# Six head blocks' memory V turned by a transposing DMA instead of TensorE, in a long one-core kernel

## The chip, the cores and the metric

The kernel runs on one core of a Trainium2 chip. The metric is the device time of one execution in microseconds (us). Each kernel is run several times, in rounds beside the kernel before on the same chip. Single runs of one kernel agree within about 0.1%.

In the profiles PE is TensorE (matmuls), PEld its weight loads, DVE VectorE, ACT ScalarE, POOL GpSimd, and SP the engine (SyncE) whose queue issues most DMAs. A q after an engine's name, as in SPq, means its sequencer, which waits, branches and issues DMAs. PSUM is the memory that the matmuls here write to (tiles psP, psO, psS, psU, psR), SBUF the one that holds the other on-chip tiles.

## The reference, cut to what matters

The program computes two independent things and joins them: a state-space layer (A) and a recurrent attention with memory (B). Only B matters here.

```python
for s in range(n_seg):                       # 64 segments of 32 rows
    h = jnp.concatenate([mem, xs], axis=1)   # 8 memory rows and 32 rows of x
    q, k, v = h @ Wq, h @ Wk, h @ Wv         # 32 heads of 128
    p = softmax(mask(q @ k.T * scale))
    o = (p @ v) @ Wo
    mem = o[:, :M, :]                        # memory of the next segment
    outs.append(o[:, M:, :])
```

The kernel doesn't walk through the 64 segments. It guesses all memory rows first (73 distinct ones in all), computes all segments at once, and checks the guess at the end. If the check failed, a slow general loop would run; it is in the program as a branch that is skipped in these runs.

## The kernel before

The 32 heads are worked in 16 pairs (`hp`), and V in 8 blocks of four heads (`hb`). V of the x rows is computed in the first phase and kept in DRAM (`vx`). V of the 73 memory rows is computed by `v_mem`: for blocks 0 and 1 at the end of the second phase, for blocks 2 to 7 inside the attention phase.

```python
def v_mem(self, hb, w=None):
    k = self.k
    w = w or self.load_wv(hb)
    p = k.ps("P")
    for h in range(4):
        for c in range(KC):
            k.PE.matmul(p[:, h * NM:(h + 1) * NM], w[:, c, h * 128:(h + 1) * 128], self.memT[:, c, :], start=(c == 0), stop=(c == KC - 1))
    vm = self.vmp.tile([128, 4, NM], BF16, name="b_vm", bufs=1)
    k.copy("v", vm[:], p[:, 0:4 * NM].rearrange("p (h n) -> p h n", h=4))
    yield
    pt = k.ps("P", (128, 1024), BF16)
    for h in range(4):
        k.PE.transpose(pt[0:NM, h * 128:(h + 1) * 128], vm[:, h, :], k.ident[:])
    st = self.next_st()
    k.copy("v", st[0:NM, 0, :, 0:E], pt[0:NM, 0:512].rearrange("p (h e) -> p h e", h=4))
    sv = st[:, 0, :, :].rearrange("p h e -> p (h e)")
    k.SP.dma_start(self.vx[hb][64:64 + NMX, :], sv[0:NMX, :])
    k.SP.dma_start(self.vt[hb][:], sv[NMX:NM, :])
    yield
```

The result lies with the head's 128 elements on the partitions and must be turned, so that the rows can be stored. TensorE does it, four transposes a block. In the attention phase the steps of this generator are interleaved with the rest, and the V tile of the next head pair is loaded from DRAM some way behind:

```python
for n, (hp, u) in enumerate(at):                 # at: attention, 11 steps u for each head pair
    ...
    if hp % 2 == 0 and 2 < hp + 2 < HP:
        if u == 4:
            vm = b.v_mem(hp // 2 + 1)
        if u in (4, 6):
            next(vm)
    ...                                          # projections of the next pair are mixed in here
```

## Time and profile before

| | before |
|---|---|
| time, median of 3 runs (lowest to highest) | 1247.11 us (1246.69 to 1247.39) |
| span of the profiled execution | 1245.3 us |
| TensorE (PE) busy | 1234.2 us, 99% |
| VectorE (DVE) busy | 667.7 us, 54% |

These are lines of the page of the kernel before: busy time of each engine, then the chain of waits that ended last, by engine and by line.

```profile
span 1245.3 us, 20124 instructions
PE 1234.2 (99%) x8270; PEld 662.5 (53%) x8342; DVE 667.7 (54%) x1250; ACT 263.4 (21%) x631; POOL 275.8 (22%) x407
...
PE 99%; issue 0%; DVE 0%
```

TensorE is the limit nearly everywhere. In the ten windows of 50 us from 550 to 1050 us it is busy 499.74 of 500 us.

What does one group of transposes cost? The timeline of PE around the first of the six groups says it (start in us, length in us, engine, line, operation, tiles, shape, count):

```profile
570.71 0.33 PE L64 MATMUL psO<-b_v,b_m 128*128 128x129 bf16 x3
570.88 0.39 PE L64 MATMUL psP<-ident,b_vm 128*73 128x128 bf16 x4
571.10 1.55 PE L64 MATMUL psP<-b_xe,b_wk 128*128 128x201 bf16 x16
```

The lengths overlap: four transposes of 219 ns each take 0.39 us together. The starts don't overlap: from 570.88 to 571.10 is 0.22 us for four transposes.

The queue of SP in the same stretch, kernel before (one row is one DMA's issue, waits included):

```profile
566.98 0.54 SPq L64 DMA_DIRECT2D b_wq<-in_B_Wq_dram  x1
568.82 0.39 SPq L64 DMA_DIRECT2D b_wk<-in_B_Wk_dram  x1
571.92 0.30 SPq L64 DMA_DIRECT2D b_vx<-b_vst  x1
572.27 0.32 SPq L64 DMA_DIRECT2D b_vt<-b_vst  x1
572.64 0.30 SPq L64 DMA_DIRECT2D b_tn<-b_ob  x1
572.98 0.40 SPq L64 DMA_DIRECT2D b_wv<-in_B_Wv_dram  x1
589.03 2.01 SPq L64 DMA_DIRECT2D b_on<-b_ob  x2
```

After 573.4 us the queue does nothing until 589.0 us: there is room.

### The profile page before, as it was taken

What the parts mean: (1) busy time and instruction counts of PE and PEld (TensorE: products, weight loads), DVE (VectorE), ACT (ScalarE), POOL (GpSimd) and SP (SyncE); (2) the same over time, 40 slices, a digit from 0 to 9 for tenths busy, and PEclk for the clock granted to TensorE, in tenths of its full rate; (3) what the DMA queues carried; (4) which work ended last, traced back from release to release, by engine and by line L of the source; (5) the groups of instructions that cost most, each with busy time, mean ns of one, the idle gap of its engine ahead of it and who ended that gap; (6) DMA issues with size and microseconds to landing.
All of it is one profiled execution on the core that took longest, in us unless ns stands there. A gap on an engine that the chain in (4) does not pass through costs nothing.

```text
span 1245.3 us, 20124 instructions
## 1 busy us (share of the span) xinstructions
PE 1234.2 (99%) x8270; PEld 662.5 (53%) x8342; DVE 667.7 (54%) x1250; ACT 263.4 (21%) x631; POOL 275.8 (22%) x407
## 2 busy tenths in 40 slices
PE   9999999999999999999999999999999999999998
PEld 5444444444455555556666656555665554446444
DVE  4688899998711124666666666666666641001000
ACT  5344444443310000211112111111211110000000
POOL 4111331212332321322222222222222220000000
PEclk9999999999999999999999999999999999999999
DMA  9965444554898734664454545545553379407000
GB/s 248 272 191 147 131 135 127 144 155 107 242 322 248 249 116 95 196 170 124 96 145 108 144 108 120 132 92 121 120 142 92 65 211 230 107 18 153 17 26 19
DMA packets 316246, 176.83 MB, mean 142 GB/s; under 512 B 138874, under 2 KB 301550, under 8 KB 316150
## 3 DMA queue, kind: packets, MB, share of 16 engines
q1 hardware_dynamic: 294054, 147.95, 47.8%
q10 hardware_dynamic: 21072, 24.38, 5.9%
q0 software_dynamic: 1024, 3.17, 0.7%
q8 instruction: 66, 1.08, 0.4%
q14 instruction: 30, 0.25, 0.1%
HBM read 89.14 MB, written 53.17 MB: 114 GB/s over the span
## 4 chain that ended last, share of the span: by engine, by line
PE 99%; issue 0%; DVE 0%
PE psP L64 82%; PE psU L64 9%; PE psS L64 3%; PE psO L64 2%; PE psR L64 2%; DVE b_xe L91 0%; DVE b_ost L91 0%; DVE a_n L962 0%; DVE hpb L105 0%; DVE ones L102 0%
## 5 line engine op out<-in xcount | busy, mean ns | idle before, releaser
L64 PE MATMUL psP<-b_xe,b_wq 128*128 128x480 bf16 (+1 forms) x1280 | 247.7, 343 | 0.1
L64 PE MATMUL psP<-b_xe,b_wk 128*128 128x480 bf16 (+1 forms) x1280 | 247.7, 343 | 0.0
L64 PE MATMUL psP<-b_wv,b_xe 128*128 128x512 bf16 (+2 forms) x1033 | 223.4, 372 | 0.8
L644 POOL TENSOR_TENSOR b_m<-b_e,maskB 99x396 bf16<-99x396 bf16 x160 | 139.8, 874 | 338.5 <-ACT b_e L641 338.5
L641 ACT ACTIVATE b_e<-psS 99x396 bf16<-99x396 f32 x176 | 88.2, 501 | 536.7 <-PE psS L64 533.4
L64 PEld LDWEIGHTS <-b_wk 128*128 128x128 bf16 x1280 | 119.4, 98 | 94.2
L64 PEld LDWEIGHTS <-b_wq 128*128 128x128 bf16 x1280 | 118.7, 98 | 87.7
L64 PEld LDWEIGHTS <-b_xe 128*128 128x128 bf16 x1056 | 101.8, 98 | 119.1 <-DVE b_xe L91 0.2
L91 DVE CAST b_k<-psP 128x480 bf16<-128x480 f32 (+1 forms) x192 | 97.4, 528 | 100.9 <-PE psP L64 100.9
L91 DVE CAST b_q<-psP 128x480 bf16<-128x480 f32 (+1 forms) x192 | 97.4, 528 | 93.1 <-PE psP L64 91.5
L64 PEld LDWEIGHTS <-b_ol 128*128 128x128 bf16 x864 | 84.3, 98 | 94.4
L64 PE MATMUL psU<-a_xT,a_bt 128*128 128x512 bf16 x493 | 113.9, 379 | 1.1
L64 PE MATMUL psP<-t,a_hl 128*128 128x512 bf16 x496 | 112.1, 379 | 0.8
L91 DVE CAST b_ost<-psP 128x512 bf16<-128x512 f32 (+1 forms) x17 | 11.5, 676 | 177.4 <-PE psP L64 176.3
L64 PE MATMUL psP<-wo,b_ol 128*128 128x512 bf16 (+1 forms) x440 | 91.9, 364 | 0.4
L64 PE MATMUL psP<-t,b_ol 128*128 128x512 bf16 x408 | 91.7, 379 | 0.4
L280 POOL TENSOR_SCALAR a_tt<-a_pr,a_tabf 128x1 f32<-128x1 f32 x48 | 34.1, 710 | 243.2 <-DVE a_pr L275 243.2
L661 DVE TENSOR_TENSOR b_ob<-psO,b_accR 99x384 bf16<-99x384 f32 x160 | 85.9, 553 | 2.4 <-DVE b_accR L660 0.4
L89 ACT ACTIVATE b_vst<-psP 128x512 bf16<-128x512 f32 x126 | 71.9, 589 | 71.3 <-PE psP L64 59.9
L267 DVE TENSOR_TENSOR a_pr<-psU,a_tabf 128x2048 f32<-128x2048 f32 x32 | 73.0, 2282 | 15.7 <-PE psU L64 14.0
L64 PEld LDWEIGHTS <-a_bt 128*128 128x128 bf16 x512 | 49.2, 98 | 57.6
L64 PEld LDWEIGHTS <-a_hl 128*128 128x128 bf16 x512 | 49.0, 98 | 56.7
(200 smaller groups left out, 962.7 us busy)
## 6 DMA issues: line engine op xcount, KB each, us to landing
b_v<-b_vx SPq DMA_DIRECT2D x16, 1122.0 KB
b_wv<-in_B_Wv_dram SPq DMA_DIRECT2D x16, 1024.0 KB
b_vx<-b_vst ACTq DMA_DIRECT2D x24, 544.0 KB
b_on<-b_ob SPq DMA_DIRECT2D x15, 720.0 KB
a_hs<-a_h SPq DMA_DIRECT2D x32, 256.0 KB
b_wog<-in_B_Wo_dram SPq DMA_DIRECT2D x4, 2048.0 KB
b_wq<-in_B_Wq_dram SPq DMA_DIRECT2D x16, 512.0 KB
b_wk<-in_B_Wk_dram SPq DMA_DIRECT2D x16, 512.0 KB
```

The costliest lines, as they stand in the source:

```text
L64: r = f(*a, **kw)
L89: self.S.activation(out, in_, ACT.Copy)
L91: self.V.tensor_copy(out, in_)
L267: V.tensor_tensor(pr[:], u[:].unsqueeze(1).to_broadcast([128, 2, 2, TB]), view(t3, [[TB + 1, 2], [TB + 1, 2], [1, TB]]), ALU.mult)
L280: G.tensor_scalar(tt[:, j:j + 1], w[:, j, TB - 1:TB], t3[:, 1, TB:TB + 1], None, ALU.mult)
L641: k.S.activation(e[:], s[0:GW, :, :, 0:GW], ACT.Exp, scale=float(E) ** -0.5, accum_out=self.accE[0:GW, i:i + 1])
L644: k.G.tensor_tensor(m[0:GW, 0:4 * GP].rearrange("p (a b q) -> p a b q", a=2, b=2)[:, :, :, 0:GW], e[:], mask[0:GW, :, :].unsqueeze(2).to_b ...
L661: V.tensor_tensor(self.ob[:, b0:b0 + n, :], o[0:GW, 0:n, 0:E], r.unsqueeze(2).to_broadcast([GW, n, E]), ALU.mult)
```

## The change

The intent is to take the 24 transposes of blocks 2 to 7 off TensorE, which is the limit, and give them to the DMA engines, which are nearly half idle (on the page of the kernel before the packets take 54.9% of the time of 16 engines, the sum of its five queues). The transposing DMA of this program reads from DRAM, so the tile is stored there first.

```diff
+        self.vmt = [k.drp.tile([E, 512], BF16, name=f"b_vmt{i}") for i in range(HB)]
 ...
-        vm = self.vmp.tile([128, 4, NM], BF16, name="b_vm", bufs=1)
-        k.copy("v", vm[:], p[:, 0:4 * NM].rearrange("p (h n) -> p h n", h=4))
+        vm = self.vmp.tile([128, 4, 128], BF16, name="b_vm", bufs=1)
+        k.copy("v", vm[:, :, 0:NM], p[:, 0:4 * NM].rearrange("p (h n) -> p h n", h=4))
+        if hb > 1:
+            k.V.memset(vm[:, :, NM:128], 0.0)
+            k.SP.dma_start(self.vmt[hb][:], vm[:].rearrange("p h n -> p (h n)"))
+            yield
+            s = self.next_st()[:].rearrange("p i h e -> p (i h e)")[:, 0:576].rearrange("p (h e) -> p h e", h=4)
+            k.V.memset(s[:, :, E:EW], 1.0)
+            k.SP.dma_start_transpose(s[:, :, 0:E], self.vmt[hb][:])
+            yield
+            k.SP.dma_start(self.vx[hb][64:64 + NMX, :].rearrange("n (h e) -> n h e", h=4), s[0:NMX, :, 0:EW])
+            k.SP.dma_start(self.vt[hb].rearrange("n (h e) -> n h e", h=4), s[NMX:NM, :, 0:EW])
+            yield
 ... (the old way stays for blocks 0 and 1; for blocks 2 to 7 the generator is advanced three times and never gets there)
-                if u in (4, 6):
+                if u in (4, 6, 8):
                     next(vm)
```

Note two things that the intent doesn't mention. The SBUF tile `b_vm` grows from 584 to 1024 bytes in each partition. And SP gets 23 instructions more (583 to 606 in the built main block; twelve DMAs and their waits).

## The prediction

> **What bounds the kernel now.** TensorE. The page gives PE 1234.2 us busy of a 1245.3 us span (99%), granted clock 0.999; the chain of waits is 99% PE. In ten 50 us windows from 550 to 1050 us (most of the attention phase) PE is busy 499.74 of 500 us, DVE 60%, POOL 27%, ACT 18%, DMA about half. In the waits of 480 to 960 us no PE row appears: DVE, ACT and POOL wait for PE, never the reverse. So PE time removed there should come off the total one for one, and nothing else should.

> **What the change removes.** For head blocks 2 to 7: four TensorE transposes each (24 in all, with their weight loads) and one 391 ns DVE copy from PSUM. The trace gives 219 ns for one transpose, but that is a pipelined length. The PE timeline shows what the group occupies: transposes start at 570.88 us, the next projection matmul at 571.10 us; the other five blocks read the same (638.45 to 638.67, and so on). So 0.22 us per block, 1.3 us in all, 55 ns per transpose. [...] Multiplying 24 by 219 ns would give 5.3 us, which I take to be wrong.

> **What it adds.** Per block, on the SP queue: a 128 KB store to DRAM, one transposing DMA that waits for it, and the two V stores cut into 272-byte instead of 1088-byte runs, waiting for the transpose. On DVE: two small memsets. The built order of PE instructions differs only by the 24 transposes; ACT and POOL are identical.

> **Is the added latency on the path?** Before, the V stores issue at 571.9 and 572.3 us, and the next V load that can read them at 592.3 us or later. Now, as an estimate: store at 567, transpose issued near 570 to 571 (a 256 KB transposing load in the first phase occupies the queue 1.3 to 1.5 us, so this one about 1 us), landing near 573 to 576; the V weight load now stands ahead of the V stores, which go out at 574 to 577 and land by about 582. The next SP work, an output store, comes only at 589.0 us because it waits for DVE. So the detour hides in some 16 us of idle queue. For blocks 6 and 7 a 1 MB transposing load (4 us of queue) stands before the V stores: out by about 852, load at 862.6. Less slack, still positive. The V tile is used only in the next head pair; a pair takes 33.8 us. Extra traffic is some 2 MB of 177 MB.

> **Predicted time.** 1247.1 - 1.3 = 1245.8 us, range 1244.8 to 1246.9 (the before runs alone spread 0.7 us). Faster by over 2%: 0.005; within 2%: 0.98; slower by over 2%: 0.015.

> **What would show each step right or wrong.** No identity-times-memory matmuls in the six blocks and PE busy lower by about 1.3 us; the attention phase shorter by the same; PE still without a wait; the V stores out before the next output store at about 589 us; no V load late.

> **What would make it wrong.** A transposing DMA that lands 15 us or more after its issue would push the output stores and the V load; PE would then idle for a DMA at the start of a head pair, in six places, blocks 6 and 7 first. Slow small-run stores would act the same way. If transposes cost PE more than the gap shows, the gain would reach at most some 5 us.

The 1.3 us is six groups at the 0.22 us from start to start in the timeline, and 1247.1 - 1.3 is the predicted 1245.8 us. The sizes behind the estimate of the detour can be read in the trace of the kernel before: of its 16 transposing loads of 256 KB (`a_bt`) twelve took 1.29 to 1.52 us of the queue and four 2.13 to 2.98 us, and by the semaphores they landed 3.4 to 6.5 us after their issue; the V stores of blocks 2 to 7 landed 1.3 to 2.8 us after theirs.

## More of the kernel before

The program ends with the branch around the general loop. All engines read the flag and branch; a hint for it is given to TensorE alone, earlier:

```python
k.tc.mark_branch_hint_location("general", "LikelyTaken", engines=[mybir.EngineType.PE])
...
f0 = nc.values_load(b.flag[0:1, 0:1], min_val=0, max_val=1)
with tc.If(f0 == 1, preferred_fallthrough_block=True, label="general"):
    with tc.For_i(0, NSEG, 1) as it:
        ...
```

One more pair of lines was there to be read before the prediction, and was not. It is the view of the source line of the closing branch (L1156), rows of SP: when it branched, and when it executed the eight semaphore instructions after it.

```profile
L1156 SPq EVENT_SEMAPHORE  x8: 17/17/17, 1243.0 to 1243.5; - x8
L1156 SPq COMPARE_BRANCH  x1: 58/58/58, 1240.1 to 1240.1; - x1
```

SP branched at 1240.1 us and executed its next instruction at 1243.0 us, 2.86 us later.

## The result, and the profile after

The changed kernel took 1244.59 us in the median of 4 runs (1244.54 to 1244.90), the kernel before 1246.99 us (1246.69 to 1247.39; now four runs). The ratio is 0.9981, with a 95% interval of 0.9964 to 0.9998. Ratios in this document are the mean time of one kernel's fast runs over that of the other's of the same rounds, so not quite the ratio of the medians quoted. The gain is 2.4 us; 1.3 us was predicted, and the range ended at 1244.8 us.

Lines of the page of the changed kernel, in the same order as above:

```profile
span 1242.8 us, 20112 instructions
PE 1232.9 (99%) x8246; PEld 660.9 (53%) x8318; DVE 668.4 (54%) x1256; ACT 263.2 (21%) x631; POOL 275.7 (22%) x407
...
PE 99%; DMA 1%; issue 0%; SPq 0%; DVE 0%
```

PE is busy 1.3 us less, as predicted, but the span is 2.4 us shorter. And a DMA has entered the chain of waits. The PE timeline of the changed kernel, where the transposes were:

```profile
571.52 0.33 PE L64 MATMUL psO<-b_v,b_m 128*128 128x129 bf16 x3
571.69 1.55 PE L64 MATMUL psP<-b_xe,b_wk 128*128 128x201 bf16 x16
```

The group is gone. But the row before it comes at a later time than in the kernel before (571.52 against 570.71 us): the changed kernel is 0.8 us late here, before it has gained anything. The SP queue of the changed kernel:

```profile
568.08 0.54 SPq L64 DMA_DIRECT2D b_vmt<-b_vm  x1
568.71 0.40 SPq L64 DMA_DIRECT2D b_wq<-in_B_Wq_dram  x1
569.63 0.39 SPq L64 DMA_DIRECT2D b_wk<-in_B_Wk_dram  x1
570.11 1.75 SPq L64 DMA_TRANSPOSE b_vst<-b_vmt  x1
571.91 0.47 SPq L64 DMA_DIRECT2D b_tn<-b_ob  x1
572.42 0.37 SPq L64 DMA_DIRECT2D b_wv<-in_B_Wv_dram  x1
575.59 0.95 SPq L64 DMA_DIRECT2D b_vx<-b_vst  x1
576.59 0.85 SPq L64 DMA_DIRECT2D b_vt<-b_vst  x1
589.62 2.07 SPq L64 DMA_DIRECT2D b_on<-b_ob  x2
```

The detour fits into the idle stretch: the V stores are out at 577.4 us, the next work comes at 589.6 us. By the semaphores in the trace, the transposing DMA landed at 575.6 us, 5.5 us after its issue. So this part went as foreseen.

Where, then, did the time go? The following table cuts each span at points that all kernels here share, read from starts in the timelines. Each row is the length of a stretch in us, good to 0.01 us (the last row's values are differences of the unrounded times). One profile of each kernel stands behind it.

| stretch | before | after | difference |
|---|---|---|---|
| start to the fourth block of V of the first eviction group (first matmul into psU with V weights) | 12.85 | 13.52 | +0.67 |
| from there to the first query projection | 458.06 | 458.04 | -0.02 |
| from there to the first matmul into psO (attention) | 21.25 | 21.40 | +0.15 |
| from there to the last matmul into psO | 528.71 | 527.36 | -1.35 |
| from there to the end of the last DVE copy | 218.87 | 218.87 | 0.00 |
| from there to the end of the span | 5.51 | 3.64 | -1.87 |

The sum is -2.42 us, the difference of the two spans. The attention phase gained what the transposes cost. Two things are left to explain, neither near the code that was changed: a loss of 0.7 to 0.8 us at the start and a gain of 1.9 us at the very end.

The end, in the changed kernel, by the same view of the closing branch as before (it is L1169 here):

```profile
L1169 SPq EVENT_SEMAPHORE  x8: 17/17/17, 1240.1 to 1241.1; - x8
L1169 SPq COMPARE_BRANCH  x1: 58/58/58, 1239.6 to 1239.6; - x1
```

SP goes on 0.5 us after its branch and not 2.9 us after. In the kernel before, the last store had landed at 1241.49 us, 1.5 us before SP went on, so it was not what SP stood still for. Nor was it the semaphore that SP's next instruction names: the last DMA of that one had landed at 1173.0 us. In the changed kernel SP does wait for the last store, until 1240.85 us, so the end gains only 1.87 us of the 2.3 us by which the stall is shorter.

The start, PE timeline, first of the kernel before, then of the changed one:

```profile
8.93 1.91 PE L64 MATMUL psP<-b_wv,b_xe 128*128 128x256 bf16 x16
```

```profile
9.60 1.91 PE L64 MATMUL psP<-b_wv,b_xe 128*128 128x256 bf16 x16 [0.36 <-DMA b_wv<-in_B_Wv_dram]
```

In brackets stands the idle time of the engine before the row and what ended it: the load of the V weights, which came later, though it was issued at the same time (2.84 to 2.85 us in both). In the changed kernel this load stands in the chain of waits, from its issue to its landing:

```profile
2.84 6.72 DMA b_wv<-in_B_Wv_dram
```

It landed at 9.56 us; in the kernel before the same load had landed at 8.70 us.

### The profile page after: what moved, and what is told of

The parts are those of the page before. It is cut to its first block, busy times and chain, and to the rows that moved or that the text cites. A ratio compares the mean times of both kernels' runs of the same rounds, so it can differ in the third digit from the quotient of the medians.

```text
span 1242.8 us, 20112 instructions
## 1 busy us (share of the span) xinstructions
PE 1232.9 (99%) x8246; PEld 660.9 (53%) x8318; DVE 668.4 (54%) x1256; ACT 263.2 (21%) x631; POOL 275.7 (22%) x407
## 3 DMA queue, kind: packets, MB, share of 16 engines
q0 software_dynamic: 1024, 3.17, 0.7%
## 4 chain that ended last, share of the span: by engine, by line
PE 99%; DMA 1%; issue 0%; SPq 0%; DVE 0%
PE psP L64 82%; PE psU L64 9%; PE psS L64 3%; PE psO L64 2%; PE psR L64 2%; DMA b_wv<-in_B_Wv_dram 1%; SPq L64 0%; DVE b_ost L91 0%
```

## The experiments

Theory A. The transposes cost 1.35 us, as their spacing says. The rest of the difference is a matter of places: the stall after SP's branch is a fetch of instructions, which depends on where in SP's instruction stream the branch stands; the late load at the start comes from the moved SBUF tiles.

Rival B. The transposes, with their PSUM slot and their DVE copy, were worth more than their spacing shows, up to the whole 2.4 us, and the two ends are chance.

Each experiment was run in 5 rounds beside the kernel before. One table for all, in us; the stretches are those of the table above.

| run | median | before, same rounds | start | to query projection | to psO | attention | to last DVE copy | end |
|---|---|---|---|---|---|---|---|---|
| before | 1246.99 | | 12.85 | 458.06 | 21.25 | 528.71 | 218.87 | 5.51 |
| the change | 1244.59 | 1246.99 | 13.52 | 458.04 | 21.40 | 527.36 | 218.87 | 3.64 |
| e1 transposes twice | 1248.23 | 1246.92 | 12.89 | 458.04 | 21.26 | 530.04 | 218.88 | 5.42 |
| e2 change, dead transposes | 1246.25 | 1246.92 | 13.63 | 458.03 | 21.57 | 528.71 | 218.88 | 3.74 |
| e3 SP plus 2 | 1246.96 | 1246.92 | 12.97 | 458.04 | 21.27 | 528.71 | 218.88 | 5.39 |
| e4 SP plus 6 | 1244.95 | 1246.92 | 13.12 | 458.03 | 21.13 | 528.71 | 218.87 | 3.46 |
| e5 SP hint | 1246.97 | 1246.72 | 12.60 | 458.97 | 21.12 | 528.71 | 218.88 | 5.46 |
| e6 change, SP hint | 1244.87 | 1246.72 | 13.76 | 458.03 | 21.28 | 527.36 | 218.88 | 3.64 |
| e7 change, SP plus 105 | 1246.54 | 1246.72 | 13.66 | 458.46 | 21.41 | 527.35 | 218.88 | 5.26 |
| e8 wide memory V tile | 1247.81 | 1246.72 | 13.73 | 458.04 | 21.39 | 528.71 | 218.88 | 5.37 |
| e9 change, aligned | 1244.06 | 1247.12 | 12.75 | 458.90 | 21.13 | 527.35 | 218.88 | 3.68 |
| e10 change again | 1244.71 | 1247.12 | 13.51 | 458.04 | 21.60 | 527.35 | 218.88 | 3.63 |

All gave correct results.

### e1: the transposes twice

```diff
-        for h in range(4):
+        for h in list(range(4)) * (2 if hb > 1 else 1):
             k.PE.transpose(pt[0:NM, h * 128:(h + 1) * 128], vm[:, h, :], k.ident[:])
```

> The kernel before, with each of the 24 transposes of head blocks 2 to 7 issued twice; nothing else moves (SP, DVE, ACT and POOL orders are identical). Theory A: the transposes cost their pipelined spacing, 55 ns each, 0.22 us a block, and the rest of the gain of the change (2.4 us measured) came from the end of the program, where SP stood still 2.86 us after its branch in the kernel before and 0.53 us in the changed one. It expects +1.3 us against before (1248.3 us) and the stretch from the end of the last DVE copy to the end of the span unchanged at 5.5 us. Rival B: the removed transposes (with their PSUM slot) were worth the whole 2.4 us; it expects +2.4 us (1249.4 us).

Measured: 1248.23 us, ratio 1.0009 (0.9995 to 1.0022). The PE timeline shows eight transposes in 0.45 us:

```profile
570.91 0.61 PE L64 MATMUL psP<-ident,b_vm 128*73 128x128 bf16 x8
571.36 1.55 PE L64 MATMUL psP<-b_xe,b_wk 128*128 128x201 bf16 x16
```

The attention stretch grew by 1.33 us, and the end stayed (5.42 us). This is A's number. The interval of the times alone would not decide between +1.3 and +2.4 us; the stretch does.

### e2: the change, with the transposes as dead work

```diff
             yield
+            pt = k.ps("P", (128, 1024), BF16)
+            for h in range(4):
+                k.PE.transpose(pt[0:NM, h * 128:(h + 1) * 128], vm[:, h, 0:NM], k.ident[:])
             s = self.next_st()[:]...
```

> The changed kernel, with the 24 TensorE transposes put back as dead work (their result is not read); SP and DVE orders are those of the changed kernel. Theory A expects +1.3 us against the changed kernel, that is 1245.9 us or 1.1 us below before, with the short end (3.6 us after the last DVE copy) kept. Rival B expects the gain to be gone: the time of before, 1247.0 us.

Measured: 1246.25 us, ratio 0.9993 (0.9980 to 1.0007), a little slower than A's 1245.9 us but 0.7 us below before. The attention stretch is back at 528.71 us, that of the kernel before to a hundredth, and the short end stayed. So the detour of DMAs cost the attention phase nothing, and the removed work gained it 1.35 us, no more. The DVE copy, which e2 doesn't put back, was worth nothing there. Rival B is out, by the stretch: the times alone lie between the two theories. The table bears this out: the stretch is 528.71 us in all six profiles with the 24 transposes done once, and 527.35 to 527.36 us in all five without them.

### e3 and e4: two and six more instructions on SP, in the kernel before

```diff
+PADS = {(3, 7): 1, (5, 7): 1}                    # e3; in e4 {(3, 7): 2, (5, 7): 2, (7, 7): 2}
 ...
+            for _ in range(PADS.get((hp, u), 0)):
+                tc.keep_in_program_order(k.SP.dma_start(b.scr[b.npad:b.npad + 1, :], b.x[0][b.npad:b.npad + 1, 0:512]))
+                b.npad += 1
```

> The kernel before, with two more instructions on SP: copies of 1 KB from DRAM to DRAM in the idle stretch of two head pairs. PE, DVE and ACT orders as before. Theory A, sharpened by where the trace shows instruction fetches of SP (near its instructions 81, 337 and 465, so 128 apart, the next near 593; the branch of the kernel before is SP's instruction 589, that of the changed one 612): with 591 the branch still stands before the next fetch point, the stall of 2.8 us after it stays, time as before (1247.0 us, within 0.4). Rival B: no change either.

> As the run before this one, with six such copies: the branch becomes SP's instruction 595, past the fetch point near 593. Theory A expects the stall after the branch to fall from 2.86 to about 0.5 us and the time to fall by about 1.9 us, to 1245.1 us, with all 32 transposes in place. Rival B: SP has nothing to do with it, time as before (1247.0 us).

Measured: e3 1246.96 us, ratio 1.0001 (0.9988 to 1.0015); e4 1244.95 us, ratio 0.9983 (0.9970 to 0.9997). The views of the branch (L1162 in both), first of e3, then of e4:

```profile
L1162 SPq EVENT_SEMAPHORE  x8: 17/17/17, 1243.0 to 1243.6; - x8
L1162 SPq COMPARE_BRANCH  x1: 58/58/58, 1240.3 to 1240.3; - x1
```

```profile
L1162 SPq EVENT_SEMAPHORE  x8: 17/17/17, 1240.8 to 1241.6; - x8
L1162 SPq COMPARE_BRANCH  x1: 58/58/58, 1240.3 to 1240.3; - x1
```

Four useless copies more, the last of them 500 us before the end (at 739.1 us), and the stall after the branch falls from 2.7 to 0.5 us. Nearly the whole gain of the change (2.0 of 2.4 us) is had without touching a transpose.

### e5 and e6: the branch hint for SP too

```diff
-    k.tc.mark_branch_hint_location("general", "LikelyTaken", engines=[mybir.EngineType.PE])
-    i = k.nc.cur_bb.bb.instructions[-1]
-    k.tc.keep_in_program_order(type("Ins", (), {"ins": i}))
+    for e in (mybir.EngineType.PE, mybir.EngineType.SP):
+        k.tc.mark_branch_hint_location("general", "LikelyTaken", engines=[e])
+        i = k.nc.cur_bb.bb.instructions[-1]
+        k.tc.keep_in_program_order(type("Ins", (), {"ins": i}))
```

> The kernel before, with the branch hint that it gives to PE alone given to SP as well (one more SP instruction; the branch becomes SP's 590th, still before the fetch point near 593). Theory A (the 2.8 us after SP's branch are a fetch of the branch target's instructions) expects the stall to fall to about 0.5 us and the time by 1.9 us, to 1245.1 us. If the stall has another cause, such as the wait for the last store's landing, the hint changes nothing: 1247.0 us.

> The changed kernel with the same hint on SP. Its stall after the branch is already 0.5 us and it then waits for the landing of the last store, so theory A expects no gain: 1244.6 us, within 0.4 us. More than 0.5 us faster would mean that the fetch still costs something there.

Measured: e5 1246.97 us, ratio 1.0001 (0.9987 to 1.0015): a miss. The stall stayed:

```profile
L1157 SPq EVENT_SEMAPHORE  x8: 17/17/17, 1243.5 to 1244.0; - x8
L1157 SPq COMPARE_BRANCH  x1: 78/78/78, 1240.7 to 1240.7; - x1
```

SP did execute the hint, at 1213.2 us. But the trace has no packet of the instruction queue that SP shares with the other engines between 1107.4 and 1241.7 us, so no fetch on the hint shows. Why not stays open. The alternative that the expectation names, the landing of the last store, is not supported either: it landed at 1241.9 us, and SP went on at 1243.5 us. e6 gained nothing, as expected (1244.87 us).

### e7: the change, with the branch moved on by 105

> The changed kernel with 105 more SP instructions (110 copies of 1 KB in idle stretches of the queue, a few waits fewer), so that its branch is SP's instruction 717, exactly 128 after that of the kernel before. Theory A with fetches every 128 instructions expects the stall of about 2.8 us back and the time 1.9 us above the changed kernel, 1246.5 us (0.5 us or so more if the copies disturb). If the number of SP instructions modulo 128 does not matter, the short end stays: 1244.6 us.

The edit is that of e3 on the changed kernel, with 110 copies of 1 KB spread over twelve head pairs. Measured: 1246.54 us, ratio 0.9999 (0.9985 to 1.0013). The view of the branch (L1175):

```profile
L1175 SPq EVENT_SEMAPHORE  x8: 17/17/17, 1242.8 to 1243.3; - x8
L1175 SPq COMPARE_BRANCH  x1: 58/58/58, 1240.2 to 1240.2; - x1
```

The stall is back, 2.6 us, with the branch exactly 128 instructions behind its place in the kernel before. The attention stretch stayed short, 527.35 us. With the branch placed as in the kernel before, the change gained next to nothing in the median; this profile also lost 0.4 us on the way to the query projection (see e9).

### e8: the wide tile alone

```diff
-        vm = self.vmp.tile([128, 4, NM], BF16, name="b_vm", bufs=1)
-        k.copy("v", vm[:], p...)
+        vm = self.vmp.tile([128, 4, 128], BF16, name="b_vm", bufs=1)
+        k.copy("v", vm[:, :, 0:NM], p...)
 ... (and the transposes read vm[:, h, 0:NM])
```

> The kernel before with the SBUF tile of the memory V widened from 4 x 73 to 4 x 128 columns as in the change, and nothing else: every later tile moves by 440 bytes in each partition. It asks about the first microseconds: in both traces of kernels with the whole change the eight matmuls of the fourth first block began 0.6 to 0.8 us later (13.5 and 13.6 us) than in the traces without it (12.9 to 13.1 us). If the place of the tiles is the cause, this run shows about 13.5 us there and 0.6 us more in all (1247.6 us); if it is chance from run to run or the DRAM buffers, about 13.0 us and 1247.0 us.

Measured: 1247.81 us, ratio 1.0010 (0.9996 to 1.0023); the start took 13.73 us and the way to psO 21.39 us. Both losses of the changed kernel are here, with nothing changed but the size of one tile. The loss at the start is clear of the scatter (12.60 to 13.12 us in the six profiles with the old alignment, 13.51 to 13.76 us in the six without). The 0.15 us on the way to psO is hardly so: 21.12 to 21.27 us against 21.28 to 21.60 us. (The expectation speaks of 440 bytes; the built program shows a shift of 416.) The PE timeline at the start shows the same wait:

```profile
9.82 1.91 PE L64 MATMUL psP<-b_wv,b_xe 128*128 128x256 bf16 x16 [0.62 <-DMA b_wv<-in_B_Wv_dram]
```

### e9 and e10: the change with the tiles on their old alignment, and the change again

In the built programs the V weights' first tile starts at byte 61440 of each partition before (120 times 512) and at 61856 after, which is no multiple of 512. Likewise the turned x: 86528, a multiple of 512, and 86944. (These addresses are of the built program, not of a trace.) One unused tile of 96 bytes makes the shift 512.

```diff
         self.vmp = c
+        self.pad = c.tile([128, 48], BF16, name="b_pad")
```

> The changed kernel with an unused SBUF tile of 96 bytes in front of the memory V's tile. The wider memory V tile (of 1024 bytes a partition in place of 584) moved all later tiles of the left side by 416 bytes in each partition, and the start addresses of the V weights, the output weights and the turned x, multiples of 512 before, were not so any more; with the 96 bytes the shift is 512 and they are again. PE, DVE, ACT, POOL and SP orders are those of the changed kernel. If the alignment is what cost 0.7 us at the start (run with the wide tile), the eight matmuls of the fourth first block begin near 12.9 us again and the time is 0.7 to 0.9 us below the changed kernel, 1243.8 us, faster than both. If it is the shift as such, the start stays at 13.6 us and the time at 1244.6 us.

> The changed kernel itself once more, in the same rounds as the aligned one, so that the two can be compared on one chip: 1244.6 us, the fourth first block's matmuls at 13.5 us, the stall after SP's branch 0.5 us.

Measured: e9 1244.06 us (1243.63 to 1244.49), ratio 0.9974 (0.9961 to 0.9988); e10 1244.71 us (1244.54 to 1245.16), ratio 0.9981 (0.9967 to 0.9995). Of the same rounds, the means of e9 and e10 are 1244.07 and 1244.78 us, ratio 0.9994. The start of e9:

```profile
8.84 1.91 PE L64 MATMUL psP<-b_wv,b_xe 128*128 128x256 bf16 x16
```

The wait for the weights is gone, and the way to psO is 21.13 us again. The packets of the trace say in part how. In the first 11 us there are 1,024 packets of 512 bytes, those of the load that TensorE waited for. Their mean time was 27.0 to 27.3 ns in the six profiles with the tiles aligned and 31.4 to 31.6 ns in the six with them not, some 16% more. This explains only a part of the delay: by an estimate from these numbers, if the packets spread evenly, 64 on each of the 16 DMA engines that the page counts, 4.5 ns longer each makes 0.29 us of the 0.86 us by which the load landed late. The rest is not accounted for. The V weights' load issued before it, at 1.74 us, had landed late already (7.04 against 6.42 us). The side of these loads that lost its alignment is the SBUF side, which is written; by what mechanism that costs time is not shown. Nor do these runs tell whether a multiple smaller than 512 bytes would have been alignment enough: only starts at a multiple of 512 and 416 bytes above one were run.

e9 is the fastest kernel, 3.1 us below before in the medians of its rounds. In its one profile (of the slowest of its five runs, 1244.49 us) it lost 0.9 us again between the start and the query projection, where TensorE waited 0.7 us for an eviction of the first phase, so in this trace the gain of the start is not kept. The same wait appears in e5 (0.8 us, its slowest run too) and smaller in e7 (0.3 us), which have little else in common with it, so it is put down to none of the changes; its cause was not looked for.

## Why the prediction was right or wrong

- **TensorE bounds the kernel, and its time comes off one for one: right, in the attention phase.** That stretch became 1.35 us shorter. Doubling the work (e1) cost 1.33 us and putting it back (e2) 1.35 us.
- **55 ns a transpose, not 219 ns: right.** The prediction read it from the starts in the timeline, 0.22 us for four. Measured, 1.35 us over 24 is 56 ns. The measured lengths of 219 ns would have meant 5.3 us.
- **The detour is hidden: right.** The V stores were out 12 us before the next work of the queue, in block 6 at 849.9 us before a V load at 862.4 us. The sizes were a little low: the transposing DMA occupied the queue 1.4 to 1.7 us (about 1 us predicted), and a V store of small runs 0.83 to 0.95 us, against 0.3 us in the kernel before.
- **"So PE time removed there should come off the total one for one, and nothing else should": wrong in its second half.** This is the step that failed. It took the change for its intent and summed only what happens near the edited lines. Two things came in from elsewhere. The end of the program became 1.87 us shorter, since 23 more SP instructions moved SP's closing branch past a point near its instruction 593, probably one of instruction fetch (e3, e4, e7). The start and the way to psO became 0.82 us longer, since a tile that grew moved all later tiles of its side by 416 bytes and took the V weights and the turned x off their 512-byte alignment (e8, e9); 0.15 us of it is hardly clear of the scatter. -1.35 - 1.87 + 0.82 is -2.40 us, and 2.4 us was measured. "PE still without a wait" failed there too: PE waited 0.36 us for the load at the start. Where the branch fell was luck, and so was it that the two effects partly cancel and leave the total near the forecast.
- **The range, 1244.8 to 1246.9 us: wrong by 0.2 us.** The only reason given for it is the run-to-run spread; it had no room for a moved branch or a moved tile.

How firmly is the fetch shown? That the stall depends on the place of the branch in SP's stream is shown: four instructions switch it off, and a shift of 128 against the kernel before brings it back. That it is a fetch is supported and not proved. Between 1236 and 1250 us the instruction queue of these engines (q14) has three packets in the kernel before and two in the changed one:

```profile
q14 instruction: 3, 0.02, 0.5%
```

```profile
q14 instruction: 2, 0.02, 0.5%
```

So it is in all twelve profiles: three packets start after SP's branch in each of the six with the stall, two in each of the six without. In those six the packet due near instruction 593 had come before the branch (at 1150.5 us in the changed kernel, 1235.1 us in e4). Which of the packets are SP's is not recorded: two start within SP's stall in the kernel before (1241.3 and 1241.4 us, with SP going on at 1243.0 us), but two follow the branch in the changed kernel also (1240.6 and 1240.9 us). The hint changed nothing (e5: 1246.97 us), and that stays open. The cost is what was measured: 2.6 to 2.9 us from SP's branch to its next instruction in the kernels with the stall, 0.5 us in those without.

## What to carry to other kernels

When a change of a few microseconds is to be judged, cut both spans into stretches at points that both kernels share, and account for each stretch, start and end included. Here twelve new DMAs and their waits moved SP's later instructions by up to 23 places, and a larger tile moved every later tile of its side by 416 bytes. So look at the end of the program for an engine that stands still after a branch with nothing to wait for (here SP, 2.86 us), and see whether a large DMA target has lost its alignment (here, to multiples of 512 bytes: 31.4 to 31.6 instead of 27.0 to 27.3 ns for a packet of 512 bytes). Here these two effects, 1.87 us one way and 0.82 us the other, stood beside the 1.35 us that the change was about.
